# A 16-point FFT factor on four-channel blocks in a kernel of long convolution, gate and MLP

## The chip, the cores and the metric

The kernel runs on one core of one Trainium2 chip. The metric is device time in microseconds from the first to the last instruction of that core, taken over several executions; the executions of one kernel lie within about 2.5% of their median here. A run that is more than 1.5% above the fastest of its kernel is called slow and is left out of ratios. All ratios below are those of the record: the mean time of one kernel's fast runs over the mean of the other's fast runs of the same rounds, on the same chip. They are therefore not quite the ratio of the medians that stand beside them, and not all of them can be had back exactly from the runs listed: for the changed kernel the listed fast runs give 628.93/604.71 = 1.040 where the record has 1.048 (1.036 to 1.060). A ratio below 1 means faster than the kernel before.

In the profile TensorE is PE (its weight loads PEld), VectorE DVE, ScalarE ACT, GpSimd POOL, and SP the sync engine, on whose queue most transfers are issued. SBUF is the memory that all engines work on, PSUM the small one that TensorE writes its results to; an eviction is the copy from PSUM to SBUF by ScalarE or VectorE. `slab` is the name of the one SBUF tile from which all buffers are cut, so it says nothing of which buffer is meant. A ring is a set of buffers used in turn.

## The reference

One forward pass and the gradients of all inputs, for a sequence of 2048 tokens with 512 channels in bf16:

```python
xn = _layernorm(x)
# A: a causal convolution as long as the sequence, by FFT of length 4096
kv  = conv4(k, shift_k) * v
kv_f, kf_f = rfft(pad(kv, 2S)), rfft(pad(ssm_k, 2S))
y   = irfft(kv_f * kf_f)[:S] + kv * ssm_D
s   = xn * y
# B: a gated MLP with a hidden width of 1376
h   = sigmoid(xn @ w_gate) * (xn @ w_up)
out = x + s * silu(h @ w_down)
# returned: out and the vector-Jacobian products of all inputs for grad_out
```

(cut and shortened from the reference; conv4 is its loop over four shifted copies)

## The kernel before

The FFT is done in two factors on TensorE. The first (`step1`) contracts over the 128 partitions. Then the 16 x 8 block of a channel octet is transposed (`flip`) so that the second factor, of 16 points, becomes a contraction over partitions as well (`step3`). The spectra are multiplied on VectorE (`cmul`) and go back through `inv3` and `inv1`. Real and imaginary parts are separate tiles, so the small transform is four matmuls of 512 columns, and a complex product is four VectorE instructions.

```python
def flip_dma(Qg, Qf):                      # backward: the flip is a DMA transpose
    for c in range(2):
        nc.sync.dma_start_transpose(Qf[:, c], Qg[:, c].rearrange("p g j e -> p (g j e)"))

def step3(Qf, qq, dst):
    ...
    nc.tensor.matmul(ps[:, 0], BD[:, 0, :], qre, start=True, stop=False)
    nc.tensor.matmul(ps[:, 0], BD[:, 1, :], qim, start=False, stop=True)
    nc.tensor.matmul(ps[:, 1], BD[:, 2, :], qre, start=True, stop=False)
    nc.tensor.matmul(ps[:, 1], BD[:, 0, :], qim, start=False, stop=True)
    nc.evac(dst, ps[:], 1024)              # ScalarE or VectorE, whichever the order gives it to

def cmul(X, K, out, conj):
    T1, T2 = out, t2_r.next()
    nc.vector.tensor_tensor(out=T1, in0=K, in1=X[:, 0:1, :].to_broadcast([P, 2, 512]), op=ALU.mult)
    nc.vector.tensor_tensor(out=T2, in0=K, in1=X[:, 1:2, :].to_broadcast([P, 2, 512]), op=ALU.mult)
    ...                                    # and two sums of 512 elements
```

The forward's last stream, per group of 128 channels, in four blocks `qq`. Its spectra are also stored to DRAM (`KK_d`) for the backward pass:

```python
for qq in range(5):
    if qq < 4:
        Xc = Xc_r.next()                   # a ring of two buffers
        yield from step3(QfV, qq, Xc)
        nc.gpsimd.dma_start(KK_d[cg, qq, 1], Xc)
        ys[qq] = Yc_r.next()
        cmul(Xc, KFg[...qq...], ys[qq], False)
    if qq > 0:
        yield from inv3(ys.pop(qq - 1), qq - 1, Bg)
```

The MLP weights are transposed for the backward pass by DMA, issued on the sync queue while the forward's last groups run:

```python
nc.sync.dma_start_transpose(wdT[:, :, 0:F], B_w_down)
for w, src, dst in ((wg, B_w_gate, wgT), (wu, B_w_up, wuT)):
    nc.sync.dma_start_transpose(dst[:, 0:NFB - 1, :], src[:, 0:128 * (NFB - 1)])
    ...
```

And the kernel's streams are merged into one fixed order of instructions for each engine by a small list scheduler inside the program, with a cost table of its own. At run time each engine takes its instructions strictly in that order.

## Time and profile before

| | before |
|---|---|
| time | 603.85 us median of 3 runs (600.78 to 609.5) |
| span of the profiled run | 604.4 us, mean granted clock 0.974 |
| PE, DVE, ACT, POOL busy | 90%, 71%, 53%, 25% |
| forward (to the last inverse transform) | 174.1 us |
| MLP backward (to its last token block) | 226.7 us |
| backward convolution and weight gradients | 203.6 us |

I split the span at two marks: the end of the last eviction of `inv1` in the forward, and the end of the last token block of the MLP backward. The lines of the profile that carry the reading are in the prediction.

### The profile page before, as it was taken

How to read it: one execution, taken by the hardware profiler on the slowest of the kernel's cores; microseconds unless marked ns; L12 is line 12 of the kernel's file. 1: busy time of each engine (PE TensorE's matmuls, PEld its weight loads, DVE VectorE, ACT ScalarE, POOL GpSimd, SP SyncE). 2: the span in 40 equal slices, each digit the busy share in tenths (PEclk: the TensorE clock that was granted, in tenths of full speed). 3: DMA queues.
4: the chain of work that ended last, by engine and by line, in shares of the span. 5: the costliest groups of instructions: out<-in, count | busy, mean ns of one | idle time of the engine just before them, and what ended most of it. 6: DMA issues, size and time to landing. Idle time of an engine off the chain costs nothing.

```text
span 604.4 us, 12639 instructions
## 1 busy us (share of the span) xinstructions
PE 545.8 (90%) x5129; PEld 371.2 (61%) x5129; DVE 430.7 (71%) x863; ACT 320.8 (53%) x428; POOL 150.9 (25%) x259
## 2 busy tenths in 40 slices
PE   4978899988799979899989998979989989999996
PEld 3866778776476556565667665544655655665634
DVE  7799998644658976889878789521849878569350
ACT  7879999768553433334335434323746655544411
POOL 2322242412111312212312111310314252331211
PEclk9979999999979989999999999998999998999999
DMA  8976888699957775888885789999797969985461
GB/s 228 268 194 214 257 210 215 173 154 212 272 140 171 197 201 149 219 156 229 196 236 151 184 228 278 216 249 274 198 221 228 272 203 291 212 281 195 138 189 37
DMA packets 160484, 125.91 MB, mean 208 GB/s; under 512 B 108627, under 2 KB 141225, under 8 KB 160426
## 3 DMA queue, kind: packets, MB, share of 16 engines
q1 hardware_dynamic: 143482, 71.32, 51.2%
q0 software_dynamic: 16416, 53.78, 30.6%
q8 instruction: 40, 0.66, 0.5%
q14 instruction: 18, 0.15, 0.1%
q10 hardware_dynamic: 528, 0.00, 0.0%
HBM read 52.79 MB, written 46.11 MB: 164 GB/s over the span
## 4 chain that ended last, share of the span: by engine, by line
PE 42%; DVE 24%; DMA 15%; ACT 8%; issue 8%; POOL 2%; POOLq 0%; DVEq 0%; ACTq 0%
PE psum L479 42%; DVE slab L479 24%; ACT slab L479 8%; DMA slab<-slab 8%; DMA KK_d<-slab 3%; DMA slab<-in_grad_out_dram 2%; DMA out_dram<-slab 1%; POOL out_dram L479 1%; POOL slab L479 1%; DMA slab<-in_A_k_dram 1%; POOL KK_d L479 0%; POOLq L1381 0%; DVEq L479 0%; POOL sF_d L479 0%; POOL hF_d L479 0%
## 5 line engine op out<-in xcount | busy, mean ns | idle before, releaser
L479 PE MATMUL psum<-slab 128*128 128x128 bf16 (+5 forms) x5129 | 545.8, 269 | 53.2 <-ACT slab L479 26.1
L479 PEld LDWEIGHTS <-slab 128*128 128x128 bf16 (+2 forms) x5129 | 371.2, 100 | 227.4 <-issue 42.6
L479 DVE TENSOR_TENSOR slab<-slab 128x512 bf16<-128x512 bf16 (+5 forms) x551 | 300.8, 586 | 42.2 <-ACT slab L479 24.8
L479 ACT CAST slab<-psum 128x1024 bf16<-128x1024 f32 (+4 forms) x245 | 201.5, 855 | 176.5 <-PE psum L479 143.4
L479 POOL DMA_DIRECT2D out_dram<-slab x75 | 44.2, 592 | 220.2 <-DVE slab L479 138.1
L479 DVE TENSOR_TENSOR slab<-psum,slab 128x512 bf16<-128x512 f32 (+2 forms) x68 | 44.4, 654 | 35.9 <-PE psum L479 21.8
L479 ACT COPY slab<-psum 128x1024 bf16<-128x1024 bf16 (+1 forms) x65 | 53.1, 830 | 28.2 <-PE psum L479 27.9
L479 ACT ACTIVATE slab<-psum 128x512 bf16<-128x512 f32 (+1 forms) x64 | 37.3, 583 | 50.4 <-PE psum L479 50.0
L479 ACT ACTIVATE slab<-slab 128x512 bf16<-128x512 bf16 (+3 forms) x51 | 40.3, 802 | 22.4 <-DVE slab L479 21.8
L479 DVE CAST slab<-psum 128x1024 bf16<-128x1024 f32 (+1 forms) x12 | 14.1, 1178 | 30.7 <-PE psum L479 27.2
L479 POOL DMA_DIRECT2D KK_d<-slab x32 | 20.3, 639 | 55.8 <-ACT slab L479 41.7
L479 DVE SCALAR_TENSOR_TENSOR slab<-slab 128x1 f32<-128x1 f32 (+3 forms) x64 | 28.0, 437 | 4.1 <-ACT slab L479 2.8
L479 POOL DMA_DIRECT2D slab<-in_A_q_dram x29 | 16.6, 572 | 45.1 <-ACT slab L479 21.5
L479 DVE SCALAR_TENSOR_TENSOR slab<-psum,slab 128x512 f32<-128x512 f32 x16 | 11.0, 689 | 18.1 <-PE psum L479 18.1
L479 POOL DMA_DIRECT2D slab<-KK_d x16 | 11.6, 725 | 29.2 <-DVE slab L479 29.2
L479 DVE TENSOR_SCALAR slab<-slab 128x1 f32<-128x1 f32 (+8 forms) x49 | 16.7, 357 | 1.7 <-ACT slab L479 1.0
L479 DVE COPY slab<-psum 128x1024 bf16<-128x1024 bf16 (+1 forms) x15 | 10.1, 671 | 9.0 <-PE psum L479 8.9
L479 POOL TENSOR_TENSOR slab<-slab 128x1 f32<-128x1 f32 (+1 forms) x20 | 12.1, 603 | 12.7 <-DVE slab L479 10.7
L479 POOL DMA_DIRECT2D slab<-in_grad_out_dram x16 | 8.9, 556 | 18.2 <-DMA out_dram<-slab 13.0
L479 DVE BATCH_NORM_STATS2 slab<-slab 128x6 f32<-128x512 bf16 x16 | 11.0, 686 | 1.7 <-DMA slab<-in_A_q_dram 1.7
L479 POOL DMA_DIRECT2D slab<-slab x8 | 4.6, 574 | 27.1 <-DVE slab L479 26.3
L479 POOL DMA_DIRECT2D slab<-in_A_k_dram x12 | 10.2, 852 | 1.5 <-issue 0.7
(22 smaller groups left out, 39.9 us busy)
## 6 DMA issues: line engine op xcount, KB each, us to landing
KK_d<-slab POOLq DMA_DIRECT2D x32, 256.0 KB, 5.4
slab<-KK_d POOLq DMA_DIRECT2D x16, 512.0 KB, 8.1
out_dram<-slab POOLq DMA_DIRECT2D x58, 128.0 KB, 4.0
hS_d<-slab SPq DMA_DIRECT2D x16, 352.0 KB, 2.9
dgS_d<-slab SPq DMA_DIRECT2D x16, 352.0 KB, 3.5
duS_d<-slab SPq DMA_DIRECT2D x16, 352.0 KB, 2.8
slab<-hS_d SPq DMA_DIRECT2D x8, 512.0 KB, 4.6
slab<-dgS_d SPq DMA_DIRECT2D x8, 512.0 KB, 9.3
```

Source lines behind the costliest of these rows:

```text
L479: getattr(getattr(self.nc, eng), meth)(*[place(v) for v in a], **{x: place(v) for x, v in k.items()})
```

## The change

Its intent: put four channels instead of eight in a block, so that real and imaginary part of 16 points x 4 channels fill the 128 partitions together (partitions 0 to 63 are real, 64 to 127 imaginary). The small transform is then one contraction, two matmuls instead of four. The complex product becomes elementwise on full tiles, but needs the spectrum a second time with its halves swapped; the sums move into the inverse transform's accumulation. The swapped copy is made by two DMA transfers of 64 partitions in the forward, and by two half-partition copies on ScalarE in the backward. The backward flips go from DMA transposes to TensorE.

```diff
+    def step3(Qf, qq):
+        ps = ps_mm([1024], name="ps_x")
+        for h in range(2):
+            nc.tensor.matmul(ps[:, h * 512:(h + 1) * 512], BD, Qf[:, 8*qq+4*h : 8*qq+4*h+4, :]..., start=True, stop=True)
+        return ps
-    def cmul(X, K, out, conj): ...
+    def inv3(parts, qq, Bg):
+        for g in range(8):
+            for n, (Y, Rt) in enumerate(parts):
+                nc.tensor.matmul(ps[:, g]..., Y[:, g * 128:(g + 1) * 128], Rt, start=(n == 0), stop=(n == len(parts) - 1))
 # forward
-            for qq in range(5):
+            for qq in range(6):
+                if qq > 1:
+                    Xc, Xs = xs.pop(qq - 2)
+                    P1 = P1_r.next()
+                    nc.vector.tensor_tensor(P1, Xc, KFg[:, qq - 2], ALU.mult)
+                    nc.vector.tensor_tensor(Xs, Xs, KFg[:, qq - 2], ALU.mult)
+                    inv3([(P1, RS1), (Xs, RS2)], qq - 2, Bg)
                 if qq < 4:
-                    Xc = Xc_r.next()
-                    yield from step3(QfV, qq, Xc)
+                    ps = step3(QfV, qq)
+                    Xc, Xs = Xc_r.next(), Xs_r.next()
+                    nc.evac(Xc, ps, 1024)
+                    nc.sync.dma_start(Xs[0:64], Xc[64:128])
+                    nc.sync.dma_start(Xs[64:128], Xc[0:64])
                     nc.gpsimd.dma_start(KK_d[cg, qq, 1], Xc)
 # backward
-            flip_dma(Qg, Qf)
+            yield from flip(Qg, Qf)
...
+                    nc.scalar.copy(Xw[0:64], ps[64:128])
+                    nc.scalar.mul(Xw[64:128], ps[0:64], -1.0)
...                  # seven products and sums of 1024 elements on VectorE, three inv3 operands
 # constants: five small tables [128, 128] in place of three, generated after the large table instead of before it
```

(cut; index arithmetic shortened)

## The prediction

> **What bounds the kernel now.** I read the page's busy shares first, then busy time by stretch, then instructions by shape, then the chain of waits, and last the DMA queue of the stretch where the chain sits on a transfer. The source gives the stages: forward convolution (four channel groups through streams K, V and X) with half of the forward MLP up to about 175 us, MLP backward to about 375, then backward convolution beside the weight gradients.
>
> ```profile
> PE 545.8 (90%) x5129; PEld 371.2 (61%) x5129; DVE 430.7 (71%) x863; ACT 320.8 (53%) x428; POOL 150.9 (25%) x259
> ...
> 20.00:125.00 105.00, 96.01 (x1246) 79.84 (x1245) 91.90 (x144) 94.16 (x113) 35.28 (x60) 0.97 0.79 210
> 125.00:175.00 50.00, 40.54 (x440) 31.37 (x438) 23.84 (x45) 30.86 (x38) 7.46 (x14) 0.90 1.03 217
> ...
> 375.00:420.00 45.00, 40.42 (x279) 21.77 (x277) 15.48 (x39) 13.81 (x20) 9.79 (x16) 0.96 1.11 253
> 420.00:583.00 163.00, 155.17 (x1103) 93.02 (x1101) 117.51 (x187) 84.91 (x98) 45.95 (x69) 0.99 0.83 222
> ```
> Columns after the stretch and its length are PE, PEld, DVE, ACT and POOL busy, granted clock, DMA share, GB/s. See that from 20 to 125 us PE, DVE and ACT are all near full, that from 125 to 175 us no engine is and DMA is, and that from 420 us PE alone is near full.
>
> ```profile
> L479 PE MATMUL psum<-slab 128*128 128x512 bf16 x48 | 10.5, 379 | 0.0
> ...
> L479 PE MATMUL psum<-slab 128*128 128x128 bf16 x111 | 6.4, 219 | 0.0
> ...
> L479 ACT CAST slab<-psum 128x1024 bf16<-128x1024 f32 x157 | 155.8, 1026 | 82.0 <-PE psum L479 68.4 <-DMA slab<-slab 4.6 <-DVE slab L479 2.9
> L479 DVE TENSOR_TENSOR slab<-slab 128x1024 bf16<-128x1024 bf16 x96 | 61.8, 684 | 4.3 <-ACT slab L479 4.2
> ...
> L479 ACT CAST slab<-psum 4x512 bf16<-4x512 f32 x1 | 0.6, 575 | 2.1 <-PE psum L479 2.1
> ```
> The first two lines are dense stretches (566 to 576 and 346 to 352 us): a 512-column matmul costs 10.5/48 = 0.219 us and a 128-column one 6.4/111 = 0.058, whatever their means of 379 and 219 ns say. Weight loads hide.
>
> ```profile
> 119.26 15.84 DMA KK_d<-slab
> 380.15 16.32 DMA slab<-slab
> 398.66 9.93 DMA slab<-slab
> 433.29 15.32 DMA slab<-slab
> ...
> 114.58 22.73 SPq L479 DMA_TRANSPOSE slab<-in_B_w_gate_dram  x1
> ...
> 408.63 0.59 PE L479 MATMUL psum<-slab 128*128 128x512 bf16 x2 [3.49 <-DMA slab<-slab]
> 448.65 1.57 PE L479 MATMUL psum<-slab 128*128 128x512 bf16 x8 [3.00 <-DMA slab<-slab]
> ```
> The chain sits on a store of spectra at 119 us (the X buffers may not be refilled before it lands) while the sync queue spends 22.73 us on one weight transpose; and three times on the DMA transposes that flip the backward spectra, two of which end PE waits of 3.49 and 3.00 us.
>
> **What the Trainium skill says.** "TensorE: Matmul & The Clock Gate", Back-to-back issue gap, gives N/2.4 + 2.5 ns for an isolated warm stream (56, 109, 216 ns at N = 128, 256, 512), and about 81 and 131 ns at 128 and 512 for load-and-matmul pairs. This trace agrees with the first (58 and 219 above), not with the second, so I use the first. "ScalarE: Activation LUTs", What ACT_TABLE_LOAD costs, has one element per cycle and lane, 186 + 0.833 N ns: 1039 ns at 1024, measured 1026; a 4-partition copy took 575 ns against 585 for 128, so half the partitions save nothing. "VectorE: DVE Perf Modes", Two Vector instructions with no wait between them, says that an instruction whose operands start in another partition quadrant than before starts only when all earlier ones have finished; no run shows that yet. "DMA: Bandwidth & Descriptors", Anatomy of one DMA, gives about 2 us fixed plus the bytes; here 128 KB stores landed in 4.0 us at the median, and the store above in 15.8 on crowded queues.
>
> **The change part by part.** A spectrum is computed for each of 16 blocks (4 channel groups of 4).
>
> PE in all: by shape, 1220 x 0.216 + 3397 x 0.056 + 384 x 0.109 + 128 x 0.149 = 515 us of pure streaming, so about 90 of 604 us are real gaps. Counting in the same way the matmuls that start in each stretch, the gaps are 17 us of 20 to 125, 15 of 125 to 175, 7 of 375 to 420 and 12 of 420 to 583.
>
> Forward, PE: the small transform takes two 512-column matmuls a block, not four, for K and for V: 128 become 64, -13.8 us. The inverse takes 16 of 128 columns, not 8 of 256: 128 x 0.109 = 14.0 becomes 256 x 0.056 = 14.3, +0.4. The flips, 32 transposes a group, stay as many. Forward, DVE: two 1024-element and two 512-element products a block become two of 1024: 32 x 0.422 = 13.5 us of busy time go, about 11 of it issue time, as 512-element products follow each other in about 0.34 us. ACT keeps its evacuations. DMA gains two 128 KB half swaps a block on the sync queue, 32 in all, 4 MB.
>
> From 20 to 125 us ACT and DVE share evacuations, so relief of one serves both. About three quarters of the blocks fall there: 12 x 2 x 0.34 = 8 us, shared by two engines, 4 us of time. PE loses more than that, which only widens its gaps, except from 100 us on, where PE is the fuller: 2 to 3 us. That makes -7 by the end of this stretch. After it the queues are full of weight transposes, and the last two groups need 16 swaps through the same in-order sync queue. The buffers are two deep, so a group has two swap latencies in its path; some of that is spent already on the 15.8 us store, and I charge 2 us a group net: +4. Forward: -3 us.
>
> Backward, PE: the transform goes from 64 to 32 matmuls, -6.9; the inverse of the first product has one matmul of 128 columns for a 4-channel group, that of the second two, so 256 x 0.109 = 27.9 becomes 384 x 0.056 = 21.5, -6.4; flips come onto PE, 128 transposes x 0.056 = +7.2. Sum -6.1 us, on the engine that sets this stage. The eight flip transfers go, and with them the PE waits of 3.49 and 3.00 us: -6 us more. ACT gets two half-partition copies a block at 1.01 us, 32 us, and ACT or DVE 16 flip evacuations at 1.03 or 0.69, 11 to 16 us. DVE goes from four 1024 and four 512 products to seven of 1024 a block: 16 x (3 x 0.684 - 4 x 0.422) = +6 us of busy time; in issue steps of 0.66 and 0.34 it is +10, and quadrant changes may add 5 x 16 x 0.05 = 4. In the 163 us stretch ACT rises from 85 to about 130 and DVE from 118 to about 128. Both fit, at 80%; I charge 2 us for new waits. Backward: -10 us.
>
> Constants at the start: some fifteen more short DVE and POOL instructions, while weights load; nothing on the path, since the first transform runs at about 29 us. MLP backward is untouched.
>
> Sum: 603.85 - 3 - 10 = 591 us.
>
> **The rivals.** (1) PE is the only bound and every gap stays as it is: 13.4 + 6.1 us of streaming go, 584 us; with the flip waits, 578. For it: PE is 90% busy and the backward stage is plainly its own. Against it: DVE and ACT are at 56.48 and 57.51 of 60 us from 40 to 100 us, so PE relief there is partly idle time. (2) The swaps become the new wait: with the sync queue held for 22.73 us at a stretch, one pair of swaps in each of the last two groups could wait 8 us more than I charge, and DVE and PE, both in order, stop with them: 607 us. For it: the KK_d store took 15.84 us in just this stretch, and the in-order sync queue adds waiting before issue. Against it: the static order moves other matmuls ahead, and PE's stretch already has this gap. (3) ACT becomes the backward bound: the Xw copies hold PSUM for 3 us rather than 1 and feed two of the DVE products; if the shared evacuations all stay on ACT it is 130 us plus queueing in 163, the PE relief turns into waits on ACT: 599 us. (4) The flip transfers are hidden anyway and PE finds other gaps: 597 us.
>
> **Range and chances.** The mean of these, weighted to my own sum, is near 591, just under the 2% line of 591.8. Both signs are open in the forward tail, so the range is 578 to 605. Chances: faster 0.51, same 0.43, slower 0.06.
>
> **What would show it.** Right: 64 fewer 512-column matmuls forward and 32 fewer backward, a PE streaming sum near 495 us; no PE wait on a slab-to-slab DMA after 375 us, and the first backward transform 20 us earlier than 408; ACT about 45 us busier after 375. DVE forward about 13 us less. Wrong: DVE or PE waiting for slab-to-slab DMAs between 110 and 175 us for over 10 us (rival 2), PE waits on ACT after 420 us of over 8 us in sum (rival 3), or a stage of 20 to 125 us that shortens by 10 us or more (rival 1).

## The result, and the profile after

The changed kernel is slower: 629.18 us median (624.61 to 632.75, 4 runs) against 606.67 us (600.78 to 613.05, 4 runs of the kernel before in the same rounds). The ratio of the fast runs is 1.048, with a 95% interval of 1.036 to 1.060.

| us | before | after |
|---|---|---|
| forward | 174.1 | 205.7 |
| MLP backward | 226.7 | 223.4 |
| backward convolution and weight gradients | 203.6 | 193.7 |
| span of the profiled run | 604.4 | 622.8 |

The whole loss, and more, is in the forward: 31.6 us there, of which the two later stages give back 13.2 in these traces. The busy time by stretch says where in it. The columns are the stretch, its length, then busy time of PE, PEld, DVE, ACT and POOL with the number of instructions, the granted clock, the DMA share and GB/s. Before:

```profile
80.00:110.00 30.00, 29.18 (x381) 24.16 (x380) 24.84 (x45) 29.00 (x35) 10.89 (x19) 1.00 0.76 213
110.00:140.00 30.00, 25.99 (x331) 20.60 (x328) 19.09 (x34) 20.97 (x27) 9.54 (x17) 1.00 0.99 159
140.00:175.00 35.00, 29.41 (x291) 22.27 (x292) 16.56 (x34) 20.98 (x26) 5.61 (x10) 0.85 0.96 241
```

After:

```profile
80.00:110.00 30.00, 23.70 (x334) 19.61 (x332) 22.20 (x37) 28.23 (x35) 10.48 (x19) 1.00 0.77 247
110.00:140.00 30.00, 20.25 (x316) 18.12 (x316) 10.14 (x17) 14.49 (x20) 6.12 (x12) 0.88 1.12 153
140.00:175.00 35.00, 21.69 (x209) 15.53 (x208) 11.11 (x16) 17.70 (x21) 4.32 (x8) 0.79 0.83 209
```

From 110 us on, VectorE does 17 instructions in 30 us where it did 34, and no compute engine is over 70% busy. DMA is full: its share is 1.12 by the profile's count of packet time, while it moves only 153 GB/s. It was nearly as full before (0.99 and 159 GB/s), but now the engines wait for it. The view of waits from 20 to 205 us (engine, what it waited for, us in total, times, longest) of the changed kernel:

```profile
DVE slab L479 <- DMA slab<-slab: 38.1, 6, 14.7
...
PE psum L479 <- DVE slab L479: 34.2, 13, 10.8
...
ACT slab L479 <- DMA slab<-slab: 14.9, 4, 10.5
```

VectorE stood 38.1 us and ScalarE 14.9 us for transfers from SBUF to SBUF, in part at the same moments, and PE 34 us behind VectorE. In the kernel before neither of them waits for such a transfer in the forward. Which instructions stood is told by VectorE's groups by shape in that window (the last part of a line is idle time before the group, and what ended it):

```profile
L479 DVE TENSOR_TENSOR slab<-slab 128x1024 bf16<-128x1024 bf16 x32 | 21.4, 688 | 33.8 <-DMA slab<-slab 23.4 <-PE psum L479 7.1 <-ACT slab L479 3.2
...
L479 DVE TENSOR_TENSOR slab<-psum,slab 128x512 bf16<-128x512 f32 x17 | 11.6, 688 | 28.3 <-DMA slab<-slab 14.7 <-ACT slab L479 7.3 <-PE psum L479 6.3
```

The first line is the 32 products of the spectra: 23.4 us for swaps. Nearly all of it stands in the last two groups, in two long waits of the third group and one of 3.10 us in the fourth:

```profile
163.76 1.29 DVE L479 TENSOR_TENSOR slab<-slab 128x1024 bf16<-128x1024 bf16 x2 [7.66 <-DMA slab<-slab]
...
181.09 1.29 DVE L479 TENSOR_TENSOR slab<-slab 128x1024 bf16<-128x1024 bf16 x2 [11.09 <-DMA slab<-slab]
```

The second group of the view by shape is not the convolution at all: it is the hidden layer of the MLP, which waited 14.7 us for a buffer whose DMA transpose had not finished. Both hang on one queue, as the sync queue's own time line shows (start, duration, operation, target and source):

```profile
109.40 13.40 SPq L479 DMA_TRANSPOSE slab<-in_B_w_gate_dram  x1
122.98 1.10 SPq L479 DMA_DIRECT2D slab<-slab  x2
124.20 15.96 SPq L479 DMA_TRANSPOSE slab<-slab  x5
140.33 5.34 SPq L479 DMA_TRANSPOSE slab<-in_B_w_down_dram  x1
...
168.77 5.78 SPq L479 DMA_TRANSPOSE slab<-in_B_w_up_dram  x1
174.65 1.17 SPq L479 DMA_DIRECT2D slab<-slab  x2
```

A weight transpose holds the queue for 13.40 us; a pair of swaps follows at 122.98, then the MLP's own transpose at 124.20. In the kernel before, such a transpose stood at 112.89 us, just ahead of the weight transpose at 114.58; by the kernel's own order of issue those at 137.99 are pieces of the weights, and the MLP's next came at 151.16. Other transfers are slow beside the weight transpose, too. Transfers issued between 105 and 125 us in the changed kernel, on whichever queue (count, size, median time from issue to landing):

```profile
KK_d<-slab POOLq DMA_DIRECT2D x4, 256.0 KB, 20.2
...
slab<-slab SPq DMA_DIRECT2D x2, 128.0 KB, 14.0
slab<-in_B_w_gate_dram SPq DMA_TRANSPOSE x1, 26.8
```

The spectra stores on the GpSimd queue took 20.2 us, where nine of them took 3.7 us at the median between 60 and 100 us in the kernel before. Over the whole execution the 32 swaps took 4.2 us at the median; those two took 14.0. The chain that ended last, from 95 to 210 us, passes through just these places:

```profile
124.20 16.95 DMA slab<-slab
...
153.13 5.91 DMA slab<-slab
...
159.43 4.23 DMA slab<-slab
...
174.65 6.34 DMA slab<-slab
```

Now the part of the change that was to gain. TensorE's pure streaming time, counted by shape as in the prediction, is 495.1 us after and 514.7 before: the 19.6 us are gone, as worked out. But the gaps grew from 90 to 128 us. The clock granted to TensorE in the forward fell from 0.95 to 0.88 as well; it is 0.97 in the run below that leaves the swaps out, but no run holds it fixed, so how much of the loss passes through the clock is not shown. In the last stage the waits of PE were, first before (from 401 us), then after (from 429 us):

```profile
PE psum L479 <- DMA slab<-slab: 6.5, 2, 3.5
PE psum L479 <- ACT slab L479: 3.1, 4, 2.1
```

```profile
PE psum L479 <- ACT slab L479: 5.1, 3, 2.8
PE psum L479 <- DVE slab L479: 3.6, 7, 1.5
```

The waits for flip transfers are gone, and the new ones on ScalarE are small. The stage is 9.9 us shorter.

### The profile page after: what moved, and what is told of

Its sections match the earlier page's. It is cut to its first block, busy times and chain, and to the rows that moved or that the text cites.

```text
span 622.8 us, 13331 instructions
## 1 busy us (share of the span) xinstructions
PE 531.3 (85%) x5417; PEld 371.6 (60%) x5417; DVE 444.9 (71%) x829; ACT 359.2 (58%) x467; POOL 152.2 (24%) x264
## 4 chain that ended last, share of the span: by engine, by line
PE 38%; DVE 21%; issue 15%; DMA 11%; ACT 10%; POOL 3%; SPq 1%; POOLq 0%; DVEq 0%; ACTq 0%
PE psum L479 38%; DVE slab L479 21%; ACT slab L479 10%; DMA slab<-slab 9%; POOL out_dram L479 2%; POOL slab L479 2%; SPq L479 1%; DMA slab<-hS_d 1%; DMA out_dram<-slab 1%; DMA slab<-in_A_q_dram 1%; POOLq L1399 0%; DVEq L479 0%; ACTq L479 0%; POOLq L479 0%; POOLq L1388 0%
## 5 line engine op out<-in xcount | busy, mean ns | idle before, releaser
L479 PE MATMUL psum<-slab 128*128 128x128 bf16 (+3 forms) x5417 | 531.3, 261 | 87.0 <-DVE slab L479 43.7
L479 PEld LDWEIGHTS <-slab 128*128 128x128 bf16 (+1 forms) x5417 | 371.6, 101 | 246.3 <-issue 67.0
L479 DVE TENSOR_TENSOR slab<-slab 128x512 bf16<-128x512 bf16 (+6 forms) x505 | 301.3, 627 | 61.3 <-DMA slab<-slab 30.8
L479 ACT CAST slab<-psum 128x1024 bf16<-128x1024 f32 (+6 forms) x247 | 202.7, 859 | 129.2 <-PE psum L479 92.4
L479 ACT COPY slab<-psum 128x1024 bf16<-128x1024 bf16 (+1 forms) x86 | 72.2, 862 | 43.2 <-PE psum L479 42.8
L479 ACT ACTIVATE slab<-psum 128x512 bf16<-128x512 f32 (+2 forms) x80 | 53.1, 664 | 60.7 <-PE psum L479 55.4
L479 DVE TENSOR_TENSOR slab<-psum,slab 128x512 bf16<-128x512 f32 (+2 forms) x68 | 44.3, 654 | 36.2 <-DMA slab<-slab 14.7
L479 DVE CAST slab<-psum 128x1024 bf16<-128x1024 f32 (+1 forms) x26 | 30.2, 1160 | 10.7 <-PE psum L479 9.4
L479 POOL DMA_DIRECT2D KK_d<-slab x32 | 17.5, 546 | 78.9 <-ACT slab L479 65.2
L479 DVE SCALAR_TENSOR_TENSOR slab<-psum,slab 128x512 f32<-128x512 f32 x16 | 11.1, 691 | 23.4 <-PE psum L479 23.4
L479 DVE TENSOR_SCALAR slab<-slab 128x1 f32<-128x1 f32 (+9 forms) x54 | 18.4, 362 | 1.7 <-ACT slab L479 0.9
L479 DVE COPY slab<-psum 128x1024 bf16<-128x1024 bf16 x10 | 6.8, 687 | 12.7 <-PE psum L479 12.7
L479 POOL TENSOR_TENSOR slab<-slab 128x1 f32<-128x1 f32 (+1 forms) x20 | 12.8, 639 | 8.6 <-DMA slab<-in_A_ssm_k_dram 6.8
```

What stands on the lines that cost most here:

```text
L479: getattr(getattr(self.nc, eng), meth)(*[place(v) for v in a], **{x: place(v) for x, v in k.items()})
```

## The experiments

My theory after the result, here called W: the forward loses by waiting, on the swaps and on what the swaps push behind the weight transposes in one in-order queue; two-deep buffers let the wait through to VectorE, ScalarE and PE. Rivals: O, the new fixed order of instructions is worse by itself; Q, the swaps cost because of the queue they are issued on; and a doubt, R, whether the predicted relief of 17 us exists at all.

### Is it the wait, or the order?

**Swaps that nobody waits for.** The order of the instructions on every engine was kept exactly (compared instruction by instruction). In the first kernel the two transfers go to a scratch place in DRAM and the second product reads another operand; they still read `Xc`, so they still hold its two buffers. In the second they read a constant table and hold nothing. Their outputs are wrong, which doesn't matter for the times.

```diff
-nc.sync.dma_start(Xs[0:64], Xc[64:128])            # as planned
+nc.sync.dma_start(sw_d[cg, qq, 0], Xc[64:128])     # as emitted, same place in the order
+nc.sync.dma_start(sw_d[cg, qq, 0], Cf[...])        # second kernel
-nc.vector.tensor_tensor(Xs, Xs, KFg[:, qq - 2], ALU.mult)
+nc.vector.tensor_tensor(Xs, KFg[:, qq - 2], KFg[:, qq - 2], ALU.mult)
```

> The changed kernel with every engine's instruction order unchanged; the swap transfers are still issued at the same places but write to DRAM scratch, and the second product reads the K spectra twice, so nothing waits for a swap (wrong forward numbers on purpose). Theory W (the loss is the wait for swaps that land late): 595 to 605 us. Rival O (the order that was planned around the swaps is long in itself): 618 us or more. Both in part: between.

Measured: 625.08 us median, ratio 1.031 (1.016 to 1.047). Most of the loss stayed. ScalarE now waited 19.3 us for the transfers to DRAM that still held `Xc`, so the run did not separate the two theories; it showed that the buffer is also held by the transfer's read.

> As same_order_no_wait, but the swap transfers read a constant table, so they hold no X buffer either: neither the products nor the refilling of the two X buffers wait for a swap; order and traffic unchanged (wrong numbers on purpose). Theory W (waiting for swaps, buffer holds included): 605 to 612 us, forward end near 180 us. Rival O (planned order): still 620 us or more, forward end near 200.

Measured: 611.0 us, ratio 1.004 (0.998 to 1.010), forward 185.6 us. With the order unchanged, and as many bytes still moved (to DRAM here), freeing the buffers and the products takes back 4.4 of the 4.8 per cent. That speaks for W. In the forward it does not clear O, though. The ends of the four groups' inverses, read from the traces with the kernel's own order of instructions, are (us):

| | group 1 | 2 | 3 | 4 |
|---|---|---|---|---|
| before | 79.9 | 109.5 | 145.7 | 174.1 |
| after | 102.6 | 158.7 | 190.2 | 205.7 |
| same_order_free | 101.6 | 155.4 | 168.6 | 185.6 |
| no_swap (below) | 81.8 | 107.8 | 148.6 | 174.0 |

The first two groups are as late in the changed order when nobody waits for a swap; only the last two come about 20 us earlier. So 20.1 us of the forward's 31.6 are the waits for swaps, and 11.5 stay with the new order. What is left of VectorE's wait is the one on the MLP's transpose behind the weight transpose:

```profile
L481 DVE TENSOR_TENSOR slab<-psum,slab 128x512 bf16<-128x512 f32 x17 | 11.6, 687 | 24.9 <-DMA slab<-slab 11.6 <-ACT slab L481 7.3 <-PE psum L481 5.8
```

**An order planned on longer transfers.** The scheduler's cost table takes a swap to land about 2.4 us after its issue, by its own formula on an empty queue, and the largest weight transpose to hold the queue for 5. Perhaps the dependents simply stand too early.

```diff
 occ, d = self.dcost(alt)
+swap = alt[1] == "dma_start" and alt[0] == "sync" and alt[2][0].shape[0] == 64
+if "transpose" in alt[1] and str(alt[2][1].space) == "DRAM":
+    occ *= 2.5
-fin = pipe + 1.0
+fin = pipe + (4.0 if swap else 1.0)
```

> The changed kernel with the order of its instructions planned on longer DMA times: a swap lands 3 us later than the program's own cost table says, and a weight transpose holds the sync queue 2.5 times as long (the trace shows 13.4, 5.3 and 5.8 us where the table has 5). Nothing else is touched; the result is right. If the loss is a bad order (dependents of the swaps put too early in the in-order streams of VectorE and ScalarE), it comes back: 1.00 to 1.02. If the queue's hold with two-deep buffers is the loss itself, no order hides it: 1.03 to 1.07.

Measured: 625.55 us, ratio 1.039 (1.031 to 1.048), forward 204.4 us. This order, which expects the delays, is no better than the changed kernel's within the intervals. Perhaps two buffers leave little other work to put between; no run shows it. Deeper rings would be the direct test, but by the program's allocator SBUF has only two holes left, of 256 and 1216 bytes a partition, against 2048 for one more buffer; so that stays untried.

**No swaps at all.** The transfers are left out, the second product reads `Xc`, and the order is planned anew. Its output is wrong, which doesn't matter for the time.

```diff
-nc.sync.dma_start(Xs[0:64], Xc[64:128])
-nc.sync.dma_start(Xs[64:128], Xc[0:64])
-nc.vector.tensor_tensor(Xs, Xs, KFg[:, qq - 2], ALU.mult)
+nc.vector.tensor_tensor(Xs, Xc, KFg[:, qq - 2], ALU.mult)
```

> The swaps taken out altogether, the second product reads the unswapped spectrum, the order planned anew (numbers wrong on purpose). No engine has more to do than in the changed kernel, and nothing waits for a swap. If the swap's waits are the whole loss, the forward falls to what PE and DVE were relieved of: forward under 172 us, 0.965 to 0.98 in all. If a rest of the loss lies elsewhere (startup 4 to 5 us, more spectra in flight, the other order), the forward stays at 180 to 186 us as in same_order_free and pe_swap_fwd, 0.985 to 1.005.

Measured: 602.99 us, ratio 1.000 (0.987 to 1.013). The forward is 174.0 us, which is 31.7 less than in the changed kernel and the same as before. So the swaps, with the order that they bring, cost about 4.8% of the time, which is 29 us by the ratios; the two traced runs are 22.1 us apart (622.8 and 600.7), as the later stages are 9.6 us longer without swaps. But the run also missed my expectation for W, under 172 us and a ratio up to 0.98: without the swaps nothing is gained. I come back to that below.

### Does another engine or queue do the swap better?

**On the GpSimd queue** (rival Q):

```diff
-nc.sync.dma_start(Xs[0:64], Xc[64:128])
-nc.sync.dma_start(Xs[64:128], Xc[0:64])
+nc.gpsimd.dma_start(Xs[0:64], Xc[64:128])
+nc.gpsimd.dma_start(Xs[64:128], Xc[0:64])
```

> The 32 half swaps issued from the GpSimd queue, not the sync queue. Rival Q (the loss is waiting behind long weight transposes in the in-order sync queue before the issue): 604 to 612 us. Theory T (the transfers themselves are slow where the engines of the DMA are full): 620 to 630 us, as little is gained by another queue.

Measured: 621.16 us, ratio 1.014 (0.987 to 1.041), so unclear; the profiled run fell in the slow state. In its trace VectorE waits 23.7 us and ScalarE 15.8 us for these transfers, nearly as before (compared only roughly, as the run is slow), so these waits do not seem to come from the sync queue alone; the MLP's wait of 14.7 us is gone. The ratio lies between both expectations and its interval reaches from no loss to nearly all of it, so Q is not settled. That another queue does not free the swaps agrees with the Trainium skill, "DMA: Bandwidth & Descriptors", Issuing engines are not separate DMA queues: transfers from any engine run on the same 16 DMA engines, and another issuer saves only the sequencer's time. The stores above, which took 20.2 us to land on their own queue while a transpose ran on another, fit that too.

**On ScalarE,** straight from PSUM:

```diff
-nc.sync.dma_start(Xs[0:64], Xc[64:128])
-nc.sync.dma_start(Xs[64:128], Xc[0:64])
+nc.scalar.copy(Xs[0:64], ps[64:128])
+nc.scalar.copy(Xs[64:128], ps[0:64])
```

> Forward swap by two half copies on ACT, as in the backward; no DMA. Theory W or S: no DMA waits, but ACT, full from 40 to 110 us, gets 32 us more: 606 to 616 us, correct. If order O from swap latency were the loss this also is free of it; the two are not told apart here, only the cost of the remedy.

Measured: 610.93 us, ratio 1.000 (0.992 to 1.009). The result is right. The profiled run is slow, so its stages are not compared.

**On TensorE.** A second table with its column halves exchanged gives the swapped spectrum directly: two more 512-column matmuls and one more eviction a block.

```diff
+TB[:, 5] = TB[:, 0] with column halves exchanged        # two small copies
-nc.sync.dma_start(Xs[0:64], Xc[64:128])
-nc.sync.dma_start(Xs[64:128], Xc[0:64])
+nc.evac(Xs, step3(QfV, qq, BDs), 1024)
```

> No swap by transfer in the forward: a second pair of 512-column matmuls with a column-swapped table makes the swapped spectrum, with one more evacuation of 1024 a block. PE +6.9 us, evacuations +16 us over two engines, no DMA. Theory W: 592 to 602 us, correct. If evacuations bind the forward stage harder than I think: 605 to 612 us.

Measured: 602.84 us, ratio 0.998 (0.982 to 1.014), forward 185.0 us; right result. Both ways of keeping the swap off DMA bring back the whole loss but nothing more.

### What do the swaps collide with?

**Weights loaded instead of transposed.** In both kernels the three weight transposes become plain loads of as many bytes. Their outputs are wrong, which doesn't matter for the times.

```diff
-nc.sync.dma_start_transpose(dst[:, 0:NFB - 1, :], src[:, 0:128 * (NFB - 1)])
+nc.sync.dma_start(dst[:, 0:NFB - 1, :], B_w_down[0:128 * (NFB - 1), :].rearrange("(fb p) d -> p fb d", p=P))
```

> The changed kernel with the three weight transposes of the sync queue replaced by plain loads of the same size (wrong numbers on purpose), so that no long transposes stand in the sync queue between 110 and 180 us. Theory S (the swaps and the MLP transposes behind them are held by the weight transposes): 608 to 614 us, 15 to 20 us less than the changed kernel, against at most 5 us less for the same edit on the kernel before. Rival (swap latency as such): 622 us or more.

Measured on the changed kernel: 606.24 us, ratio 0.998 (0.989 to 1.007). That is 5.0% less than its 1.048.

> The same edit on the kernel before: 600 to 606 us, since its spectra wait only once, 15.8 us, on a store among these transposes and other work fills most of that.

Measured on the kernel before: 595.25 us, ratio 0.978 (0.969 to 0.987). So the transposes cost 2.2% before the change and about 5% after it: by this pair some 2.8% of the 4.8% are the meeting of the two, with intervals of about 1% on each ratio. The loads still fill the DMA engines (share 1.01 from 110 to 140 us after the change), and the changed kernel still waits for swaps; its forward is 186.8 us against 162.1.

**Weights transposed on TensorE, with right results.** All three matrices already lie in SBUF in the other layout, so 132 transposes of 128 columns and 18 evictions can replace the transfers.

```diff
-nc.sync.dma_start_transpose(...)                       # three weights
+for f0 in range(0, NFB, 2):
+    pt = ps_tr([nb, 4, 128])
+    for b in range(nb):
+        for db in range(4):
+            nc.tensor.transpose(pt[:, b, db, :], blk(f0 + b, db), ident)
+    nc.evac(dst[:, f0:f0 + nb, :]..., pt[:], nb * 512)
```

> The changed kernel, swaps by DMA kept, with the same weight transposes on TensorE; the result is right. plainw_after was 0.998. If the swaps' loss comes from sharing the in-order sync queue with the weight transposes: 1.00 to 1.015, at least 3 per cent below the changed kernel's 1.048. If the swaps cost by themselves: 1.03 or more.

Measured: 602.51 us, ratio 0.993 (0.986 to 1.000), with the swaps still on DMA in the sync queue. The swap waits of VectorE's products fall from 23.4 to 13.6 us, and the MLP's wait of 14.7 us is gone:

```profile
L479 DVE TENSOR_TENSOR slab<-slab 128x1024 bf16<-128x1024 bf16 x32 | 21.4, 687 | 18.1 <-DMA slab<-slab 13.6 <-PE psum L479 4.2 <-ACT slab L479 0.3
```

> The kernel before with its three weight transposes made on TensorE from the copies that already lie in SBUF (132 transposes of 128 columns, 7.4 us of streaming by the 0.056 us of the trace, and 18 evictions), so no transfer holds the sync queue between 109 and 160 us. The result is right. plainw_before, with no transposes at all, was 0.978. If the queue's hold is what costs: 0.978 to 0.992. If the engines of the forward's end have no room for the transposes: 0.995 to 1.01.

Measured: 600.41 us, ratio 0.991 (0.984 to 0.999). The same edit is worth 5.5% in the changed kernel and 0.9% in the kernel before, so by this pair 4.6% are the meeting of the two, where the pair above gave 2.8%. Take the weight transposes off DMA, and the change as a whole costs nothing that the intervals can show: 0.993 against 0.991. The stages do not tell this by themselves: the forward is still 185.6 us against 161.1, but the MLP backward 220.0 against 241.4. Why the one shrinks where the other grows is not shown.

### What is the relief worth?

**Backward alone.** The forward of the kernel before with the backward of the changed one. The tables in it are slices of another constant, so the gradients are wrong; instructions and sizes are right.

```diff
 # the kernel before, with
+    step1_n, flip_n, step3_n, inv3_n            # step1, flip, step3, inv3 of the changed kernel, for the backward only
+    BDn, RH, RC1, RS2 = (Cf[:, 0, q, :] for q in range(4))   # stand-ins for the new tables
-    frontC, backC of the kernel before
+    frontC, backC of the changed kernel
```

> The forward convolution of the kernel before, the backward of the changed one (numbers of the backward wrong on purpose, same shapes and counts). Theory W (the swaps of the forward are the whole loss, the backward gains its predicted 10 us or a little more): 590 to 598 us, ratio to before 0.975 to 0.985. Rival B (the backward loses too, through the two half copies on ACT or the flips on PE): 606 us or more.

Measured: 608.47 us, ratio 1.004 (0.989 to 1.019). The predicted gain did not show. Repeated with more rounds:

> The kernel of bwd_only once more, in five rounds: the forward of the kernel before, the backward of the changed one (numbers wrong on purpose). The first look gave 1.004 with an interval of 0.989 to 1.019, where my prediction's backward gain of 10 us asks for 0.983. If the backward gain is real, 0.978 to 0.990 here; if PE's 6 us and the flip waits are given back inside the backward stage, 0.995 to 1.005. The stretch from the end of the MLP backward to the end, 203.6 us before, should be 193 to 196 if the gain is real (it was 193.8 in the changed kernel).

Measured: 606.97 us, ratio 1.007 (0.998 to 1.017). The last stage was 202.7 and 200.2 us in the two traces, against 203.6 before and 193.7 in the changed kernel, with the same instructions. In the second trace one wait stands out, first on TensorE, then on ScalarE behind it (idle time before an entry in brackets):

```profile
418.40 19.06 PE L480 MATMUL psum<-slab 128*128 128x128 bf16 x152 [7.28 <-ACT slab L480]
```

```profile
415.39 1.93 ACT L480 COPY slab<-psum 128x1024 bf16<-128x1024 bf16 x2 [6.67 <-DMA duS_d<-slab]
```

A buffer's earlier content is still being stored by DMA when the stage wants to begin. In the changed kernel, whose forward is 31 us longer, the entry at the same place shows 0.64 us. I then repeated the pair with the weight transposes on TensorE, to see whether a relieved queue lets the gain through. The edit is that of bwd_only and that of pewt_before together. Its output is wrong, which doesn't matter for the time.

> Forward of the kernel before with the weight transposes on TensorE, backward of the changed kernel (numbers wrong on purpose, as in bwd_only). pewt_before, which differs only in its backward, was 0.991 with an interval of 0.984 to 0.999. If the backward relief of about 10 us is real where the sync queue is free: 0.970 to 0.980, and the last stage 193 to 197 us against 202.1. If the relief is given back in waits at the stage's start, as in both bwd_only traces (7.3 and 8.6 us): 0.985 to 0.995, last stage 199 to 203.

Measured: 603.56 us, ratio 0.989 (0.981 to 0.996) against 0.991 for pewt_before. Again no gain that the intervals can show; the last stage is 200.5 us against 202.1. PE's waits in it:

```profile
PE psum L480 <- ACT slab L480: 9.1, 3, 4.2
PE psum L480 <- DVE slab L480: 4.1, 6, 1.6
```

In the traces of the two backward-only kernels TensorE waits 12.8, 9.9 and 9.1 us for ScalarE in this stage, where the changed kernel has 5.1. This is the kind of wait that the prediction's third rival named. Why the same code has fewer such waits when the forward is changed too, I can't say: the order of instructions was planned anew in each, and no run separates the two.

**No swaps and no weight transposes** (wrong): what the arithmetic of the change is worth where DMA is out of the way. The edit is that of no_swap and that of plainw_after together.

> No swaps and plain loads in place of the weight transposes, numbers wrong on purpose: what the change's arithmetic alone is worth where the sync queue is free. plainw_before is 0.978 and no_swap 1.000. If the predicted relief of 17 us (7 forward, 10 backward) exists but was covered by the transposes: 0.945 to 0.96. If it doesn't reach the span at all: 0.97 to 0.98.

Measured: 586.66 us, ratio 0.970 (0.961 to 0.978), against 0.978 (0.969 to 0.987) for plainw_before. It was run at another time. The difference, 0.8% or about 5 us, is less than the two intervals, and well below the 17 us. The two traces are further apart, 580.2 and 598.6 us, but they caught the fastest of four runs of the one and the slowest of the other; and the forward, where 7 us were predicted, is not shorter in them: 165.3 us against 162.1. DMA does explain why the stretch from 110 us stood still without any swap. First no_swap, then noswap_plainw:

```profile
110.00:140.00 30.00, 18.04 (x269) 15.62 (x267) 8.46 (x14) 18.79 (x25) 8.85 (x17) 0.93 1.17 165
```

```profile
110.00:140.00 30.00, 26.18 (x387) 22.77 (x388) 15.91 (x27) 26.42 (x33) 10.71 (x22) 1.00 0.89 282
```

With the transposes in place, 30 us hold 269 matmuls and DMA moves 165 GB/s at a share of 1.17; without them 387 matmuls and 282 GB/s.

### The start, and a version that beats both

The forward of the changed kernel also begins late. TensorE's first long run, before and after:

```profile
11.07 6.76 PE L479 MATMUL psum<-slab 128*128 128x128 bf16 x64 [1.29 <-ACT slab L479]
```

```profile
16.83 11.00 PE L479 MATMUL psum<-slab 128*128 128x128 bf16 x160 [1.54 <-ACT slab L479]
```

The first K spectra are flipped at 30.3 us instead of 26.4. The cause is on ScalarE, which evicts the first transposes and in the fixed order stands behind the sine of the new small tables:

```profile
15.48 0.83 ACT L479 ACTIVATE slab<-slab 128x640 f32<-128x640 int32 x1 [0.82 <-DVE slab L479]
```

In the kernel before, the sine of the small tables ran at 6.91 us, ahead of the large one. Moving the small tables' code ahead of the large table's loop, on top of pe_swap_fwd:

```diff
+    ... angles of the small tables, tri = Sin(an)      # the same lines, moved up
     for h in range(2):                                 # the large table
         ...
         nc.scalar.activation(Cf[:, :, js], mc[:, :, js], ACT.Sin, bias=negpi, scale=sc)
-    ... angles of the small tables, tri = Sin(an)
     nc.vector.tensor_tensor(TB[:, 0], tri[:, 0], mask[:, 0], ALU.mult)
```

> Candidate to beat both. The swapped spectra of the forward come from TensorE (a table with its column halves exchanged, two more 512-column matmuls and one more eviction a block, as in pe_swap_fwd, which was 0.998), and the small tables are generated before the large one, so that ScalarE does not hold for them at 15 us. The startup was 4 to 5 us later in the changed kernel. If the startup delay stays in the span: 0.985 to 0.993. If the forward absorbs it: 0.995 to 1.003, as pe_swap_fwd.

Measured: 604.04 us, ratio 1.003 (0.996 to 1.011). The first flip comes at 28.5 us, but the forward ends at 185.0 us as in pe_swap_fwd: those 2 us are absorbed later. Then both transfers that hurt were put on TensorE, the forward swap and the weight transposes (the edits of pe_swap_fwd and pewt_after together):

> Candidate to beat both: the changed kernel with the forward swap on TensorE and the weight transposes on TensorE; the result is right. pe_swap_fwd was 0.998 and pe_swap_tf 1.003. If DMA is what ate the change's relief of PE and VectorE: 0.97 to 0.988. If the relief was never on the path: 0.99 to 1.005.

Measured: 594.21 us, ratio 0.980 (0.974 to 0.986), right result, forward 166.1 us. And with the small tables first (the edit of pe_swap_tf added):

> The best version so far (swap and weight transposes on TensorE, 0.980) with the small tables generated ahead of the large one. In the changed kernel the first K spectra were flipped at 30.3 us, against 26.4 before; with this edit 28.5 in pe_swap_tf. If those 2 us stay in the span: 0.975 to 0.978. If something later absorbs them, as pe_swap_tf against pe_swap_fwd suggests: 0.979 to 0.985.

Measured: 591.0 us (587.15 to 598.73, 6 runs), ratio 0.970 (0.962 to 0.978), right result. This is the best version: 3.0% faster than the kernel before, and about 7% faster than the changed kernel. That the table order gives the last 1% is not shown; the two versions' intervals overlap. They were run at other times. The Trainium skill, "VectorE: DVE Perf Modes", The three transpose paths, gives 390 ns for a 128x128 transpose on TensorE and 1309 ns by DMA, and under Rules for kernel authors advises TensorE where a PSUM destination will do. The runs agree in direction; in this kernel a TensorE transpose costs 0.056 us of streaming, by the prediction's count for 128 columns.

## Why the prediction was wrong

It said 591 us with a range up to 605; measured 629.18. By its own steps:

- **"I charge 2 us a group net: +4."** This is the step that failed. The forward took 205.7 us where -3 had been predicted for it, that is 171. With order and traffic kept, the waits for swaps alone are worth 20.1 us of it (205.7 against 185.6 in same_order_free, one trace of each), not 4, and swaps and their order together 4.8% of the time (1.048 against 1.000 without them). They fell where the prediction had looked, in the last two groups (7.66, 11.09 and 3.10 us on VectorE), and for the reason that rival 2 gave: the swap behind the longest wait was issued at 174.65 us, right behind a weight transpose that had held the queue for 5.78 us, and took 6.34 more. Rival 2, 16 us above the charge of 4, had this term nearly right. What nobody had counted is the rest: the new order puts one of the MLP's own transposes behind a weight transpose (14.7 us of VectorE), and 11.5 us of forward stay when nothing waits for a swap. The 158.7 us of the second group's inverse, 109.5 before, belong to this part.
- **"Over 10 us" of waits between 110 and 175 us** was the sign given for rival 2. It came: VectorE alone waited 14.72 and 7.66 us there. The larger of the two was for the MLP's transpose, not for a swap.
- **Forward, -7 us by 125 us.** Right in its counts; its size is not confirmed. TensorE's forward stream went from 128.4 to 115.2 us and VectorE's products of 512 and 1024 elements from 36.2 to 23.5 us of busy time. In no_swap the first inverse ends 1.9 us later than before and the second 1.7 us earlier, after a start that is 4 us late. From the first flip (3.6 us late at 30.0) to the second inverse, that is a relief of about 5 us.
- **"Constants at the start: nothing on the path."** Wrong for the first flip, which comes about 4 us late through ScalarE's fixed order; whether this reaches the span is not shown, as 2 us of it won back in pe_swap_tf did not. In no_swap the start and the relief nearly cancel by 110 us, and the forward ends where it did, 174.0 against 174.1 us. That the weight transposes alone hold it there is not shown: without them it ends at 165.3, and the kernel before at 162.1.
- **Backward, -10 us.** One line was misread: by the kernel's order of issue the transfer at 380.15 us is one of the MLP's own transposes, so two of the three are flips; they are the two with the PE waits, so the 6 us stand on the right lines. The counts held: the waits on flip transfers are gone, half-partition copies took 1.008 and 1.015 us against the 1.01 assumed, and the last stage shrank by 9.9 us in the changed kernel. But the kernel that has this backward alone shows no gain in time in either run (1.004, 1.007), nor does the pair with a relieved queue (0.989 against 0.991). The 2 us charged for new waits were too few there: TensorE waited 9.1 to 12.8 us for ScalarE, the kind of wait that rival 3 named. The first backward transform did not come 20 us earlier than 408 us but at 434.9, that is 5.8 us after the end of the MLP backward instead of 7.8. ScalarE's last stage grew by 34.6 us of busy time, not 45. The Trainium skill, "VectorE: DVE Perf Modes", Two Vector instructions with no wait between them, was cited for the quadrant changes, and this trace agrees: products on 64 partitions whose start quadrant changes follow each other in 0.717 us, those on 128 partitions that keep it in about 0.6.
- **The sum.** Relief of 17 us was credited; where DMA is out of the way the runs find about 5 us with an uncertainty of the same size (0.970 against 0.978), and 1.1% with right results (0.980 with the swap on TensorE against 0.991). A charge of 4 us was made for the swaps, and 20 us of forward were paid, 29 us by the ratios when the order that they bring is counted too.

What stays open: why the backward stage is 3 to 9 us shorter in kernels with the whole change (193.7 to 197.2 us) than in those with its backward alone (200.2 to 202.7); how deep a ring would have hidden the swaps; and how their cost divides between the queue, the loaded DMA engines and the two-deep rings.

## What to carry to other kernels

Before a new transfer is put on a path that passes through a ring of two buffers, look at what else its queue and the DMA engines carry in that stretch: the landing time that counts is the one beside the largest transfer there (14 to 20 us here), not the median (4.2), and a late one stops the engines where the ring comes round to it. A swap or a transpose of data that already lies in SBUF can be had from TensorE for a few matmuls and an eviction, where TensorE has gaps. And a relief of busy time is only worth what the fixed order and the next wait let through: try the relief alone, before it is added to a sum.

## What the Trainium skill lacked or had wrong

- "DMA: Bandwidth & Descriptors" says that initiating a DMA on another engine saves only the sequencer's time, "which is usually small relative to the DMA itself". For the DMA transposes here it was not small, and the page has no time for it on this chip, only cycle counts in a comparison of generations: one instruction held the sync queue for 22.73 us before and 13.40 us after (w_gate), 5.34 (w_down) and 5.78 us (w_up), and an SBUF-to-SBUF transpose behind it for 9.88 us.
- The same page does not say how much a running DMA transpose slows plain transfers of other queues: stores of 256 KB landed in 20.2 us beside it, 3.7 us otherwise. It gives transposes 261 GB/s; the w_gate transpose, 1.31 MB, took 26.8 us to land beside other traffic, which works out at 49 GB/s.
- "TensorE: Matmul & The Clock Gate", Back-to-back issue gap, puts pairs of weight load and matmul at about 81 ns for 128 columns and 131 ns for 512; dense stretches here show 58 and 219 ns. The page's formula for a single stream fits, the pair figures don't.
